# A looped TensorE program over a 256-column input ring, with one 120-row slot moved by gpsimd DMAs

## The chip, the cores and the metric

The kernel runs on one core of a Trainium2 chip. The metric is the device time of one execution in microseconds (us), lower is better. A profile shows one execution; its span is about 2 us below the measured time of the same execution.

An *engine* without a name is one of the 16 DMA engines of the profile's page; PE (TensorE), ACT (ScalarE), DVE (VectorE), POOL (GpSimd) and SP are the named ones. A *row* is the part of one SBUF partition that a DMA moves as one packet: 24,576 bytes for 64 columns of 192 bf16 channels. The trace's packet records give queue, time, duration and bytes, but no engine: which engine carried a row is always inferred here, from the 16 landings of a DMA and from its shape. "Over 4 engines" means that a DMA is written with `a` = 4 in `a c n`. The recorded texts speak of the *start* of such a gpsimd DMA, the engine on which it is taken to begin, and of moving it.

## The reference

A 1x1 grouped convolution: 512 x 512 pixels, 192 channels in 4 groups of 48. With a kernel of 1x1 it is one matrix product per group and pixel.

```python
# x: (1, 512, 512, 192) bf16, w: (1, 1, 4, 48, 48) bf16
xg = x.reshape(B, H, W, G, Cg)
out = einsum('bhwgc,gcd->bhwgd', xg, w[0, 0]).reshape(B, H, W, C)
```

100.66 MB are read and 100.66 MB are written, each byte once; the load and store queues of the kernel before fill 97.4% of the 16 engines' span with that, at 418 GB/s.

## The kernel before

Pixels lie on the partitions, `BIG` = 104 pixels ("columns") on each of 128 partitions per slot. SP loads slots into one ring of 520 columns; PE transposes four columns a "group" at a time, DVE copies the transposes to SBUF, PE multiplies, ACT writes the result over the input in the same ring, and stores go out from there on the ACT queue. A load waits for the store of the slot five before. PE's program is a Python loop, so each of its instructions exists once.

```python
BIG = 104
RCOLS = 5 * BIG
NARROW = ((0, 16), (32, 16))      # rows of the one narrow slot
NARROW_COLS = 48
NARROW_AT = (9,)
# ... cut

def transfers(ap, ring, p, c0=0, c1=None):
    c1 = c1 or p.size
    for (r0, rows, pix) in p.blocks:
        px = ap[pix:pix + rows * p.size, :]
        if p.full:
            view = px.rearrange("(p i) n -> p (i n)", p=rows)[:, c0 * C:c1 * C]
        else:
            view = px.rearrange("(c a i) n -> a c (i n)", a=4, c=rows // 4)
        yield view, ring[r0:r0 + rows, (p.at + c0) * C:(p.at + c1) * C]

# SP
for p in pieces:
    for q in pieces:
        if q.slot == p.slot - RCOLS // BIG:
            wq.wait(st_sem[q.i], st_val[q])
    for dram, sbuf in transfers(xf, ring, p):
        sp.dma_start(sbuf, dram).then_inc(ld_sem[p.i], 16)

# PE
for pair in range(NP):
    if pair + 1 < NP:
        transposes(pair + 1)
    matmuls(pair)
# ... cut
```

The narrow slot is there because the 16 engines are not equally fast (stores of 1.59 us instead of 1.476 on one of them, below). Its 32 rows go by DMAs over 4 engines, which by their shape leave the other 12 without work (no record names them); everything else is spread over all 16.

Of the kernel before, what the change touches and what calls it, by code (L numbers as in the profile page):

```python
# [6 lines left out]
BF16 = mybir.dt.bfloat16  # L7
# [4 lines left out]
C = GROUPS * CG  # L12
UC = 2 * C
# [11 lines left out]
BIG = 104  # L25
RCOLS = 5 * BIG
HEAD = (8, 20, 32)
LATE = 6
LATE_PARTS = (52, 52)
LAST_PARTS = (32, 32, 24, 16)  # L30
FULL = ((0, 128),)
NARROW = ((0, 16), (32, 16))
NARROW_COLS = 48
NARROW_AT = (9,)
NXP = 4
NXS = 3
# [3 lines left out]
class Waiter:  # L40

    def __init__(self, eng):
        self.eng = eng
        self.seen = {}
# [8 lines left out]
class Piece:  # L53

    def __init__(self, i, slot, at, g0, size, blocks, pix):
        self.i, self.slot, self.at, self.size = i, slot, at, size
        self.g0, self.g1 = g0, g0 + size // 4
        self.full = blocks is FULL
        self.blocks = []
        for (r0, rows) in blocks:  # L60
            self.blocks.append((r0, rows, pix))
            pix += rows * size
        self.pix_end = pix
        assert size % 4 == 0 and self.at + size <= RCOLS


def plan_pieces(npix):
    few = NARROW_COLS * sum(rows for _, rows in NARROW)
    at = [i for i in NARROW_AT if npix >= len(NARROW_AT) * few + 128 * (sum(HEAD) + BIG * (i + 2))]
    cols = (npix - few * len(at)) // 128  # L70
    assert cols % 4 == 0
    head = list(HEAD) if cols >= sum(HEAD) + BIG else []
    mid = cols - sum(head)
    slots = [[(BIG, FULL)]] * (mid // BIG) + ([[(mid % BIG, FULL)]] if mid % BIG else [])
    for i in at:
        slots.insert(i, [(NARROW_COLS, NARROW)])
    if head:
        slots.insert(0, [(s, FULL) for s in head])
    pieces, g, pix = [], 0, 0
    for n, parts in enumerate(slots):  # L80
        c = n * BIG % RCOLS
        for s, blocks in parts:
            pieces.append(Piece(len(pieces), n, c, g, s, blocks, pix))
            c, g, pix = c + s, pieces[-1].g1, pieces[-1].pix_end
    assert pix == npix
    return pieces


def bass_standalone__grouped__vision_kernel(nc, x, w, out):
# [3 lines left out]
    assert npix % 512 == 0, "the pixel count must be a multiple of 512"  # L93

    pieces = plan_pieces(npix)
    piece_of = {g: p for p in pieces for g in range(p.g0, p.g1)}
    NG = pieces[-1].g1
    NP = (NG + 1) // 2

# [4 lines left out]
    def groups(pair):  # L104
        return range(2 * pair, min(2 * pair + 2, NG))

    def transfers(ap, ring, p, c0=0, c1=None):
        c1 = c1 or p.size
        for (r0, rows, pix) in p.blocks:
            px = ap[pix:pix + rows * p.size, :]  # L110
            if p.full:
                view = px.rearrange("(p i) n -> p (i n)", p=rows)[:, c0 * C:c1 * C]
            else:
                view = px.rearrange("(c a i) n -> a c (i n)", a=4, c=rows // 4)
            yield view, ring[r0:r0 + rows, (p.at + c0) * C:(p.at + c1) * C]

    stores = []
    for p in pieces:
        late = pieces[-1].slot - p.slot
        parts = LAST_PARTS if late == 0 else LATE_PARTS if late < LATE else (BIG,)  # L120
        c = 0
        for n in parts if p.size == BIG and p.full else (p.size,):
            stores.append((p, c, c + n, p.g0 + (c + n) // 4))
            c += n
    st_val = {p: 16 * sum(len(p.blocks) for q, *_ in stores if q is p) for p in pieces}

    with ExitStack() as es:
        block = es.enter_context(nc.Block())
        ring = es.enter_context(nc.sbuf_tensor("ring", [128, RCOLS * C], BF16))
# [4 lines left out]
        wt = es.enter_context(nc.sbuf_tensor("wt", [128, WCOLS], BF16))  # L134
        xT_ps = es.enter_context(nc.psum_tensor("xT_ps", [128, NXP, 1024], BF16))
# [5 lines left out]
        ld_sem = [sem(f"ld{p.i}") for p in pieces]  # L141
        st_sem = [sem(f"st{p.i}") for p in pieces]
# [3 lines left out]
        e_done, fa_done = sem("e_done"), sem("fa_done")  # L146

        def columns(g):
            p = piece_of[g]
            at = p.at + 4 * (g - p.g0)  # L150
            return ring[:, at * C:(at + 4) * C]

        @block.gpsimd
        def _(gp):
            gp.memset(esel[:], 1.0).then_inc(p0_sem, 1)  # L155
            gp.memset(ident[:], 1.0).then_inc(p1_sem, 1)  # L156
            gp.wait_ge(p0_sem, 1)
            gp.affine_select(out=esel[:], in_=esel[:], pattern=[[-1, ECOLS]],  # L158
                             compare_op=AluOpType.is_equal, fill=0.0, base=ESHIFT,
                             channel_multiplier=1).then_inc(e_sem, 1)  # L160
            gp.wait_ge(p1_sem, 1)
            gp.affine_select(out=ident[:], in_=ident[:], pattern=[[-1, 128]],  # L162
                             compare_op=AluOpType.is_equal, fill=0.0, base=0,
                             channel_multiplier=1).then_inc(id_sem, 1)

        @block.sync
        def _(sp):
            wq = Waiter(sp)
            sp.dma_start(w_sb[:], wv).then_inc(w_sem, 16)  # L169
            for p in pieces:  # L170
                for q in pieces:
                    if q.slot == p.slot - RCOLS // BIG:
                        wq.wait(st_sem[q.i], st_val[q])
                for dram, sbuf in transfers(xf, ring, p):
                    sp.dma_start(sbuf, dram).then_inc(ld_sem[p.i], 16)  # L175

        @block.tensor
        def _(pe):
            wq = Waiter(pe)

            def build_weights():
                wq.wait(e_sem, 1)
                wq.wait(w_sem, 16)
                last = None
                for (tc, r, g, c0_) in WBLOCKS:
                    s0 = ESHIFT - r
                    col = WOFF[tc] + c0_
                    last = pe.matmul(o_ps[:, NOB - 1, col:col + CG], lhsT=esel[:, s0:s0 + 128],  # L188
                                     rhs=w_sb[:, g, :], start=True, stop=True, skip_group_check=True)
                last.then_inc(wb_sem, 1)  # L190

            def transposes(pair):
                wq.wait(e_done, pair - 1)
                last = None
                for g in groups(pair):
                    p = piece_of[g]
                    if g == p.g0:
                        wq.wait(ld_sem[p.i], 16 * len(p.blocks))
                    xg = columns(g)
                    for ul in range(2):  # L200
                        for tc in range(3):
                            j = ul * 3 + tc
                            last = pe.transpose(xT_ps[:, g % NXP, j * 128:(j + 1) * 128],  # L203
                                                xg[:, j * 128:(j + 1) * 128], ident[:])
                last.then_inc(t_done, 1)

            def matmuls(pair):
                wq.wait(e_done, pair + 1)
                for g in groups(pair):
                    xs = xT_sb[pair % NXS][:, g % 2 * 2 * UC:(g % 2 + 1) * 2 * UC]  # L210
                    wq.wait(fa_done, g - 1)
# [12 lines left out]
            wq.wait(id_sem, 1)  # L224
            transposes(0)
            wq.wait(wc_sem, 1)
            for pair in range(NP):
                if pair + 1 < NP:
                    transposes(pair + 1)
                matmuls(pair)  # L230

        @block.vector
        def _(dve):
# [3 lines left out]
            for pair in range(NP):  # L237
                n = len(groups(pair))
                b0 = pair * 2 % NXP
                wq.wait(t_done, pair + 1)  # L240
                wq.wait(mm_done, 2 * (pair - NXS + 1))
                dve.tensor_copy(xT_sb[pair % NXS][:, 0:n * 2 * UC].rearrange("p (g c) -> p g c", g=n),  # L242
                                xT_ps[:, b0:b0 + n, 0:2 * UC]).then_inc(e_done, 1)

        @block.scalar
        def _(act):
# [3 lines left out]
            def store():  # L250
                p, c0, c1, g1 = todo.pop(0)
                wq.wait(fa_done, g1)
                for dram, sbuf in transfers(of, ring, p, c0, c1):
                    act.dma_start(dram, sbuf).then_inc(st_sem[p.i], 16)  # L254

            for g in range(NG):
                wq.wait(mm_done, g + 1)
                v = 2 * g
                dst = columns(g).rearrange("p (u c) -> p u c", u=2)
                act.copy(dst, o_ps[:, v % NOB:v % NOB + 2, 0:UC]).then_inc(fa_done, 1)  # L260
                while todo and todo[0][3] <= g:
                    store()
            while todo:
                store()
            for p in pieces:
                wq.wait(st_sem[p.i], st_val[p])
# [28 lines left out]
```

## Time and profile before

485.38 us, median of 4 executions (485.06 to 485.62).

| what | value | where on the profile |
|---|---|---|
| span | 483.3 us | first line |
| load queue, store queue, instruction queue | 48.7%, 48.7%, 0.6% of 16 engines' span | part 3 |
| PE busy | 431.3 us, 89% | part 1 |
| PE waiting for loads | 21.1 us in 8 waits | wait list |
| the last chain of work | PE 54%, DMA 39% | part 4 |

These are lines of the profile's page: busy times, busy tenths in 40 equal slices of the span, GB/s per slice, the DMA queues (packets, MB, share of 16 engines) and the chain that ended last.

```profile
span 483.3 us, 13933 instructions
...
PE 431.3 (89%) x6262; PEld 392.1 (81%) x6262; DVE 250.2 (52%) x262; ACT 392.6 (81%) x522; POOL 1.3 (0%) x8
...
PE   5699999999999999998599999979998999999910
...
DMA  8999999999999999999999999999999999999993
GB/s 351 431 406 421 449 425 421 422 424 442 434 428 419 425 420 439 425 434 424 431 434 437 424 431 428 432 431 426 434 428 428 430 424 422 439 416 427 429 390 156
...
q10 hardware_dynamic: 4360, 100.67, 48.7%
q1 hardware_dynamic: 3416, 100.68, 48.7%
q8 instruction: 50, 0.82, 0.6%
...
PE 54%; DMA 39%; ACT 1%; issue 1%; SPq 0%; ACTq 0%
```

Between the first slice and the last two the engines are busy in every slice, at 406 to 449 GB/s. That is a kernel at its DMA limit. And from the wait list (waited for: us in total, times, longest):

```profile
PE xT_ps L203 <- DMA ring<-in_x_dram: 21.1, 8, 6.8
```

PE has little slack, but some: it waits for data, not data for it.

The trace also records every DMA packet with its start and duration. A row of 39,936 bytes takes 1.476 us in this kernel, and one of 24,576 bytes 0.912 us in the changed one (medians), which fits a few nanoseconds plus 0.03676 ns per byte. One engine takes about 8% longer for each row that it stores (1.587 us in the median instead of 1.476; which one, no record says). Chained by their times, the packets follow each other without gaps, so the time is the work of the engine that ends last (the prediction's chains end between 467 and 483.2 us of the 483.3).

### The profile page before, as it was taken

Reading aid. Unit: us, or ns where it says so; the run is one execution under the profiler, and the core shown is the slowest. Engines: PE = TensorE matmul, PEld = TensorE weight load, DVE = VectorE, ACT = ScalarE, POOL = GpSimd, SP = SyncE. Lnnn points to the kernel's source line nnn. Section 1 sums busy time; section 2 is a strip of 40 time slices with the busy share of each in tenths; the row PEclk is TensorE's granted clock in tenths of the full one; section 3 lists DMA queues with packets and bytes.
Section 4 is the critical chain, followed back from the end, with each engine's and each line's share of the span. In section 5 each row is a group of like instructions: output and inputs, shape, how many; then the busy total and the mean of one; then the engine's idle time right before and its main releaser. Section 6 shows DMA issues by size and latency. Waiting matters only on the chain.

```text
span 483.3 us, 13933 instructions
## 1 busy us (share of the span) xinstructions
PE 431.3 (89%) x6262; PEld 392.1 (81%) x6262; DVE 250.2 (52%) x262; ACT 392.6 (81%) x522; POOL 1.3 (0%) x8
## 2 busy tenths in 40 slices
PE   5699999999999999998599999979998999999910
PEld 5599888898898889887588988969787898899800
DVE  2345655656555565564256555544554655556500
ACT  2669999999999999998299999877888999999920
POOL 1000000000000000000000000000000000000000
PEclk9979999999999999999799999998999999999965
DMA  8999999999999999999999999999999999999993
GB/s 351 431 406 421 449 425 421 422 424 442 434 428 419 425 420 439 425 434 424 431 434 437 424 431 428 432 431 426 434 428 428 430 424 422 439 416 427 429 390 156
DMA packets 7834, 202.23 MB, mean 418 GB/s; under 512 B 1056, under 2 KB 1056, under 8 KB 1696
## 3 DMA queue, kind: packets, MB, share of 16 engines
q10 hardware_dynamic: 4360, 100.67, 48.7%
q1 hardware_dynamic: 3416, 100.68, 48.7%
q8 instruction: 50, 0.82, 0.6%
q14 instruction: 8, 0.07, 0.0%
HBM read 100.68 MB, written 100.66 MB: 417 GB/s over the span
## 4 chain that ended last, share of the span: by engine, by line
PE 54%; DMA 39%; ACT 1%; issue 1%; SPq 0%; ACTq 0%
PE o_ps L218 31%; PE xT_ps L203 22%; DMA ring<-in_x_dram 20%; DMA out_dram<-ring 19%; ACT ring L260 1%; SPq L175 0%; ACTq L254 0%; SPq L169 0%
## 5 line engine op out<-in xcount | busy, mean ns | idle before, releaser
L260 ACT CAST ring<-o_ps 128x768 bf16<-128x768 f32 x521 | 391.3, 802 | 68.5 <-PE o_ps L218 61.0
L242 DVE COPY xT_sb<-xT_ps 128x1536 bf16<-128x1536 bf16 (+1 forms) x261 | 249.6, 956 | 206.0 <-PE xT_ps L203 206.0
L218 PE MATMUL o_ps<-wt,xT_sb 128*128 128x144 bf16 (+1 forms) x3126 | 292.0, 236 | 5.9 <-ACT ring L260 1.3
L218 PEld LDWEIGHTS o_ps<-wt,xT_sb 128*128 128x128 bf16 x3126 | 212.0, 99 | 43.4 <-ACT ring L260 30.2
L203 PE MATMUL xT_ps<-ident,ring 128*128 128x128 bf16 x3126 | 222.7, 221 | 21.1 <-DMA ring<-in_x_dram 21.1
L203 PEld LDWEIGHTS xT_ps<-ident,ring 128*128 128x128 bf16 x3126 | 191.1, 99 | 22.7 <-DMA ring<-in_x_dram 19.8
L188 PE MATMUL o_ps<-w_sb,esel 48*128 48x48 bf16 x10 | 0.6, 210 | 2.7 <-DMA w_sb<-in_w_dram 2.7
L188 PEld LDWEIGHTS o_ps<-w_sb,esel 48*128 48x128 bf16 x10 | 0.5, 113 | 2.6 <-POOL esel L158 2.6
L236 DVE CAST wt<-o_ps 128x480 bf16<-128x480 f32 x1 | 0.7, 658 | 3.3 <-PE o_ps L188 3.3
L260 ACT ACT_TABLE_LOAD x1 | 1.3, 1283 | 0.8 <-PEq L280 0.8
L158 POOL TENSOR_SCALAR_AFFINE_SELECT esel<-esel 48x272 bf16<-48x272 bf16 x1 | 0.4, 405 | 0.0
L155 POOL MEMSET esel<- 48x272 bf16 x1 | 0.3, 318 | 0.3 <-POOLq L280 0.3
L162 POOL TENSOR_SCALAR_AFFINE_SELECT ident<-ident 128x128 bf16<-128x128 bf16 x1 | 0.3, 285 | 0.0
L156 POOL MEMSET ident<- 128x128 bf16 x1 | 0.2, 198 | 0.0
L280 POOL MEMSET const-bfloat16-1.0<- 128x1 bf16 x1 | 0.1, 102 | 0.0
L280 POOL MEMSET const-uint8-127<- 128x1 uint8 x1 | 0.1, 102 | 0.0
L280 POOL MEMSET const-float32-0.0<- 128x1 f32 x1 | 0.1, 98 | 0.3 <-issue 0.3
L280 POOL MEMSET const-float32-1.0<- 128x1 f32 x1 | 0.1, 98 | 0.0
## 6 DMA issues: line engine op xcount, KB each, us to landing
ring<-in_x_dram SPq DMA_DIRECT2D x19, 4992.0 KB, 37.5
out_dram<-ring ACTq DMA_DIRECT2D x13, 4992.0 KB, 45.5
out_dram<-ring ACTq DMA_DIRECT2D x10, 2496.0 KB, 47.7
out_dram<-ring ACTq DMA_DIRECT2D x3, 1536.0 KB, 19.7
ring<-in_x_dram SPq DMA_DIRECT2D x1, 1536.0 KB, 8.4
out_dram<-ring ACTq DMA_DIRECT2D x1, 1152.0 KB, 16.6
ring<-in_x_dram SPq DMA_DIRECT2D x1, 960.0 KB, 5.2
out_dram<-ring ACTq DMA_DIRECT2D x1, 960.0 KB, 28.6
```

Of the source, the lines that this page charges most:

```text
L155: gp.memset(esel[:], 1.0).then_inc(p0_sem, 1)
L156: gp.memset(ident[:], 1.0).then_inc(p1_sem, 1)
L158: gp.affine_select(out=esel[:], in_=esel[:], pattern=[[-1, ECOLS]], compare_op=AluOpType.is_equal, fill=0.0, base=ESHIFT, channel_multipli ...
L162: gp.affine_select(out=ident[:], in_=ident[:], pattern=[[-1, 128]], compare_op=AluOpType.is_equal, fill=0.0, base=0, channel_multiplier=1) ...
L188: last = pe.matmul(o_ps[:, NOB - 1, col:col + CG], lhsT=esel[:, s0:s0 + 128], rhs=w_sb[:, g, :], start=True, stop=True, skip_group_check=True)
L203: last = pe.transpose(xT_ps[:, g % NXP, j * 128:(j + 1) * 128], xg[:, j * 128:(j + 1) * 128], ident[:])
L218: last = pe.matmul(o_ps[:, v % NOB, c0_:c1_], lhsT=xs[:, j * 128:(j + 1) * 128], rhs=wt[:, WOFF[tc]:WOFF[tc] + (c1_ - c0_)], start=(tc == ...
L236: dve.tensor_copy(wt[:], o_ps[:, NOB - 1, 0:WCOLS]).then_inc(wc_sem, 1)
L242: dve.tensor_copy(xT_sb[pair % NXS][:, 0:n * 2 * UC].rearrange("p (g c) -> p g c", g=n), xT_ps[:, b0:b0 + n, 0:2 * UC]).then_inc(e_done, 1)
L260: act.copy(dst, o_ps[:, v % NOB:v % NOB + 2, 0:UC]).then_inc(fa_done, 1)
L280: nc = _bacc.Bacc("TRN2", target_bir_lowering=False, num_devices=1)
```

## The change

Intent: give PE a short program that is looped, so that PE's instructions are not fetched all the time by the same DMA engines (50 packets of 16,384 bytes here, 0.966 us in the median, the row after each about 0.4 us longer); separate the input ring from the output ring (each 4 slots of 64 columns), so that a load waits for the transposes rather than for a store; and replace the old narrow slot by one of 120 rows, which 15 engines are to carry and the slow one is not.

To leave one engine out, gpsimd DMAs are used. Slot 17 is made of DMAs over 4, 3 and 8 engines, twice (rows 0-15, 20-31 and 64-95; then 32-47, 52-63 and 96-127), and between the first and second of each three a small copy, the *spin*, is to shift the engines of the next DMA by one, past the slow one.

```diff
-BIG = 104
-RCOLS = 5 * BIG
-NARROW = ((0, 16), (32, 16))
-NARROW_COLS = 48
-NARROW_AT = (9,)
+SLOT = 64
+NSLOT = 4
+LAP = NSLOT * SG
+NARROW = 17
+NARROW_ROWS = ((0, 16, 4), (16, 0, 1), (20, 12, 3), (64, 32, 8),   # (first row, rows, a); 0 rows: spin
+               (32, 16, 4), (48, 0, 1), (52, 12, 3), (96, 32, 8))
...
+            for s in slots:                       # gpsimd
+                if not s.narrow:
+                    continue
+                wq.wait(t_done, 8 * (s.n - NSLOT + 1))
+                for dram, sbuf in narrow_parts(xf, ring_in, s):   # dram: "(c a i) n -> a c (i n)", a = engines
+                    if dram is None:
+                        wq.wait(spin_sem, 16 * spins)
+                        spins += 1
+                        gp.dma_start(spin[0:1, 0:64], xf[0:1, 0:64]).then_inc(spin_sem, 16)
+                    else:
+                        gp.dma_start(sbuf, dram).then_inc(nl_sem, 16)
+                wq.wait(nl_sem, 16 * NDMA)
+                gp.sem_inc(ld_sem[s.n % NSLOT][0], 16)
+                wq.wait(mm_done, s.g1 + 2)
+                ... the same again for the store of the slot
...
-            for pair in range(NP):
-                if pair + 1 < NP:
-                    transposes(pair + 1)
-                matmuls(pair)
+            with pe.Fori(0, NLAP):
+                for pair in range(LAP // 2):
+                    if pair:
+                        pe.wait_ge(e_done, pair)
+                    nxt = (pair + 1) % (LAP // 2)
+                    ...
+                    transposes(nxt, (2 * nxt, 2 * nxt + 1))
+                    matmuls(pair, (2 * pair, 2 * pair + 1))
+                pe.sem_inc(e_done, -(LAP // 2))
+                pe.sem_inc(fa_done, -LAP)
```

## The prediction

> **What bounds the kernel.** DMA, all 16 engines. The page's queue table gives loads 48.7%, stores 48.7% and instruction fetch 0.6% of the 16 engines' span: 98% of 483.3 us busy, 418 GB/s. The compute engines have slack: PE 431 us busy, ACT 391, DVE 250; the wait list shows PE waiting only 21 us for loads; a pair of groups takes 1.63 us where PE runs freely (timeline), so 261 pairs need about 425 us. The trace's packet records follow each other on an engine without a gap, so I could chain them (roughly) into engines: idle time is nil until an engine's last packet. From the span's start, three engines end at about 467 us, most at 475 to 478, the last ones at 480, 481 and 483.2. The time is the work of the slowest DMA engine; the mean is 476.
>
> **What makes engines unequal** (same records):
> - 50 instruction fetches of 16,384 bytes (0.88 to 1.12 us, plus about 0.4 us on the next row)[...].[...]
> - One engine stores its 39,936-byte rows in about 1.59 us instead of 1.476: an estimated 16 us over the run.
> - The old narrow slot gives 4 engines 11 us of extra work.
>
> **The change.** The PE program falls from 6262 matmults (each a weight load and a matmul) to 796, a loop body of about 1580 instructions run 8 times: [...]nearly all fetches vanish. The narrow slot now loads 15 engines and spares the slow one. Per row the engine's cost fits 5 ns + 0.03676 ns per byte (1.473 us for 39,936 bytes, 0.739 for 19,968). Ordinary engines then carry 12.61 MB, 467 us, against 462 for the three idle-early engines now: they end near 472. The slow engine carries 12.21 MB, about 10 us less: it ends near 473.5. Added: more packets (under 1 us), one or two wait instructions per pair on PE, a branch per lap[...], 16 small gpsimd DMAs. Separate rings let loads be issued when transposed instead of stored; DMA is saturated already, so that gains nothing itself. Unprofiled time is 2.3 us above the span: 476 to 478.
>
> **Two doubts.**
> 1. The loop may be fetched again each lap: [...]482 to 485.
> 2. The small "spin" DMA is lowered as 16 x 4 elements.[...] the slow engine gets the extra work too, and the time is 486 to 491. No run yet shows it.
>
> **What would show it.** Right: instruction queue below 10 packets; q1 and gpsimd rows on 15 engines, spin as one engine's packets; all engines end within 3 us of each other; DMA 9 tenths in all but the last slice; chain of waits still mostly DMA and PE. Wrong: 50 or more fetches; PE gaps of microseconds every lap; one engine running alone for 10 us at the end; PE idle not on loads but on ACT, or DMA slices below 9 near the end (output ring of 256 columns too small).
>
> I predict 478 us, range 474 to 488. Faster by over 2% (below 475.9) 0.28, within 2% 0.66, slower 0.06.

The sum: the slow engine's end, 473.5 us, and 2.3 us of an unprofiled execution over the span make 475.8; with up to 2 us for a branch per lap, whose cost no trace gave, it came to 476 to 478. (In the changed kernel PE is idle for 0.20 and 0.19 us where its laps begin at 386.3 and 439.8 us.) Cut from the first doubt is how the fetches spread over the engines. The traces give their total: 50 fetches of 0.966 us and 0.398 us (medians) on the row after each are an estimated 68 us of engine time, 4.3 us on each engine if all 16 share it. Cut from the second doubt is the reason why the spin might not pass over the slow engine, and then "the slow engine gets the extra work too"; it came from no trace.

## The result, and the profile after

498.5 us, median of 4 executions (496.26 to 501.31); 485.38 us before on the same chip. The ratio is 1.0274, with a 95% interval of 1.0228 to 1.0321: slower. (A ratio is the mean time of one kernel's fast runs over that of the other's of the same rounds, so it is not quite the ratio of the medians quoted.) The prediction's range ended at 488.

The same lines of the page, for the changed kernel; POOL's busy tenths and the gpsimd queue q0 are new. The profiled execution is the slowest of the four, 501.31 us.

```profile
span 499.6 us, 13884 instructions
...
PE 429.4 (86%) x6172; PEld 390.8 (78%) x6172; DVE 246.8 (49%) x258; ACT 389.1 (78%) x514; POOL 10.2 (2%) x24
...
PE   4999999999988899886830999972999999999995
...
POOL 1000000000000000210000021000000000000000
...
DMA  8999999999999999999999789999799999999986
GB/s 326 426 412 426 439 421 429 437 437 425 429 437 434 424 431 437 431 413 419 419 394 372 306 317 339 406 411 405 293 392 429 434 429 435 427 426 428 425 343 274
...
q1 hardware_dynamic: 5104, 97.73, 47.3%
q10 hardware_dynamic: 5616, 97.72, 46.1%
q0 software_dynamic: 1088, 5.90, 3.1%
q8 instruction: 6, 0.10, 0.1%
...
PE 8%; ACT 3%; issue 0%; ACTq 0%
```

Three things stand out. The instruction queue fell from 50 packets to 6, all of them between 19 and 64 us, so the loop is not fetched again each lap. The loss is in one place: the slices of 12.5 us from number 21 to 30 (250 to 375 us) show 293 to 411 GB/s where 420 to 440 is usual, while slot 17 is loaded and stored. And in the first of them (394 and 372 GB/s) DMA still shows nine tenths and more: the engines are busy but move less. PE runs out of input at about that time ("6830", numbers 19 to 22 of its row), and only after that do the engines run dry ("78", numbers 23 and 24). At the store it is the same again: PE's "72" in 27 and 28, the engines' "7" in 29.

The wait list gives the second half of it.

```profile
POOL ring_in L186 <- PE xT_ps L242: 199.5, 1, 199.5
...
PE xT_ps L242 <- issue: 28.9, 6, 21.6
POOL spin L184 <- DMA spin<-in_x_dram: 17.5, 1, 17.5
PE o_ps L257 <- ACT ring_out L313: 15.0, 17, 12.0
...
ACT ring_out L313 <- DMA out_dram<-ring_out: 12.4, 1, 12.4
```

The gpsimd loads are issued from 201.5 us on and have all landed only at 275.1 us (semaphore landings of the trace), 73.6 us later; the ordinary slots of this kernel land 35.0 us after their issue (median). PE stands for 21.6 us in one piece before slot 17 (the list calls it "issue", because gpsimd and not a DMA raises that semaphore). Later ACT waits 12.4 us for slot 17's store before it may write slot 21, and PE 12.0 us for ACT. From 346 us on PE has no pause over 0.3 us, and the end is now PE's: its last matmul ends at 494.3 us, 4 us before the last store row (498.7), where in the kernel before 21 us lie between the two (461.0 and 482.3). The engines stay busy until about 475 us and have too little to do after that (343 and 274 GB/s). The chain that ended last does not tell this: it breaks off after 11% of the span, here and in most kernels with two rings, e5 and e20 among them.

An account of the loss can be made from the packet records: for each stretch, 16 engines times its length, less the recorded packet time, is *idle*; recorded packet time less 8 ns and 0.03676 ns per byte of each packet is *excess*, that is, slowness. In undisturbed stretches of this kernel both are near zero (within 3 engine-us in 20 us).

```
changed kernel, engine-us        excess   idle
200 to 275 us (load of slot 17)    62.9   -4.1
275 to 350 us (its store)          75.9  106.7
350 to 375 us                      30.5   52.9
200 to 375 us                     169.3  155.5
```

So the engines lose about 325 engine-us, 20 us each, half because their packets are slow and half because they have nothing to do. Most of the slowness is in ordinary rows: of the 169.3 engine-us of excess 116.5 are in the SP loads, 27.4 in the ACT stores and 25.4 in the gpsimd rows, of which 74 of 240 take over 0.95 us. The experiments ask for the cause of each half.

### The profile page after: what moved, and what is told of

The parts are those of the page before. It is cut to its first block, busy times and chain, and to the rows that moved or that the text cites. A ratio compares the mean times of both kernels' runs of the same rounds, so it can differ in the third digit from the quotient of the medians.

```text
span 499.6 us, 13884 instructions
## 1 busy us (share of the span) xinstructions
PE 429.4 (86%) x6172; PEld 390.8 (78%) x6172; DVE 246.8 (49%) x258; ACT 389.1 (78%) x514; POOL 10.2 (2%) x24
## 5 line engine op out<-in xcount | busy, mean ns | idle before, releaser
L313 ACT CAST ring_out<-o_ps 128x768 bf16<-128x768 f32 x513 | 387.9, 801 | 105.2 <-PE o_ps L257 86.1
L290 DVE COPY xT_sb<-xT_ps 128x1536 bf16<-128x1536 bf16 x257 | 246.1, 958 | 243.2 <-PE xT_ps L242 243.2
L257 PE MATMUL o_ps<-wt,xT_sb 128*128 128x144 bf16 (+1 forms) x3078 | 286.4, 236 | 20.5 <-ACT ring_out L313 15.0
L242 PE MATMUL xT_ps<-ident,ring_in 128*128 128x128 bf16 x3084 | 220.1, 222 | 41.6 <-issue 28.9
L242 PEld LDWEIGHTS xT_ps<-ident,ring_in 128*128 128x128 bf16 x3084 | 189.7, 100 | 44.3 <-issue 44.2
L186 POOL DMA_DIRECT2D ring_in<-in_x_dram x6 | 3.5, 594 | 199.5 <-PE xT_ps L242 199.5
L196 POOL DMA_DIRECT2D out_dram<-ring_out x6 | 3.4, 563 | 70.7 <-PE o_ps L257 70.7
L184 POOL DMA_DIRECT2D spin<-in_x_dram x2 | 1.0, 514 | 17.5 <-DMA spin<-in_x_dram 17.5
L194 POOL DMA_DIRECT2D spin<-in_x_dram x2 | 1.0, 510 | 8.2 <-DMA spin<-in_x_dram 8.2
## 6 DMA issues: line engine op xcount, KB each, us to landing
out_dram<-ring_out POOLq DMA_DIRECT2D x2, 768.0 KB, 23.9
```

The source lines that it names most:

```text
L184: gp.dma_start(spin[0:1, 0:64], xf[0:1, 0:64]).then_inc(spin_sem, 16)
L186: gp.dma_start(sbuf, dram).then_inc(nl_sem, 16)
L194: gp.dma_start(spin[0:1, 0:64], xf[0:1, 0:64]).then_inc(spin_sem, 16)
L196: gp.dma_start(dram, sbuf).then_inc(st_sem[s.n], 16)
L242: last = pe.transpose(xT_ps[:, g % NXP, j * 128:(j + 1) * 128], xg[:, j * 128:(j + 1) * 128], ident[:])
L257: last = pe.matmul(o_ps[:, v % NOB, c0_:c1_], lhsT=xs[:, j * 128:(j + 1) * 128], rhs=wt[:, WOFF[tc]:WOFF[tc] + (c1_ - c0_)], start=(tc == ...
```

## The experiments

Eighteen kernels were run. All gave the right result except e15. All times are of fast runs where nothing else is said (the state of e15's single run is unknown), beside the kernel before on the same chip at 485.1 to 485.5 us. The expectations name theories by letters: **G**, gpsimd DMAs as such slow the others; **S**, the wait for the spin does it; **T**, a gpsimd DMA over few engines costs every engine many turns, so the load is late; **P**, a slot's rows are slow, and slow the rows beside them, when it is cut into DMAs that give engines other rows than a 128-row DMA does. P is the reading of shapes and durations; no record names an engine, and why such rows should be slow is not shown.

### The parts of the new slot

**e1_hw120**: the 120 rows as one 15-engine DMA on the SP queue and one on the ACT queue; no gpsimd.

```diff
-        view = ap[s.pix:s.pix_end, :].rearrange("(p i) n -> p (i n)", p=128)[:, c0 * C:c1 * C]
-        return view, ring[:, (s.at + c0) * C:(s.at + c1) * C]
+        rows = NROWS if s.narrow else 128
+        view = ap[s.pix:s.pix_end, :].rearrange("(p i) n -> p (i n)", p=rows)[:, c0 * C:c1 * C]
+        return view, ring[0:rows, (s.at + c0) * C:(s.at + c1) * C]
... (the gpsimd DMAs go; SP and ACT no longer skip the narrow slot)
```

> The narrow slot of 120 rows is loaded by one SP DMA and stored by one ACT DMA (15 engines); no gpsimd DMA is left. Theory G (the gpsimd DMAs of this slot are slow, PE waits 22 us for the load and ACT 12 us for the store, and the lead that is lost comes back as a PE-bound tail): DMA at 9 tenths in all slices, no PE wait over 7 us after the start, at most 490 us. Within theory G, if one slow-storing engine sets the end (it is not spared here): 486 to 490, all other engines done 10 us earlier; if it does not, 475 to 480. Rival R (the rings of 256 columns or the loop cost the time, not the gpsimd DMAs): 494 to 500 as in the changed kernel.

Measured: 500.64 us, ratio 1.0306 [1.0289, 1.0324]. There is no gpsimd DMA in this kernel and it is as slow as the changed one, so G is not needed to explain it. Excess while slot 17 is loaded (200 to 275 us): 52.8 engine-us. By its shape this DMA gives 120 rows to 15 engines instead of 128 to 16; which engine has which of them, no record shows. From 200 to 375 us the excess is 91.9 engine-us, against 10.1 in e5 (below): (91.9 - 10.1) / 16 = 5.1 us per engine, about half of the 10.6 us that e1 is over e5. The last engine fell up to 16 us behind the others in its loads.

**e2_no_spin**: the changed kernel without its spins and the waits for them.

```diff
-NARROW_ROWS = ((0, 16, 4), (16, 0, 1), (20, 12, 3), (64, 32, 8),
-               (32, 16, 4), (48, 0, 1), (52, 12, 3), (96, 32, 8))
+NARROW_ROWS = ((0, 16, 4), (20, 12, 3), (64, 32, 8),
+               (32, 16, 4), (52, 12, 3), (96, 32, 8))
```

> The changed kernel without its four spin DMAs; the twelve gpsimd row DMAs stay. Theory T (each tiny descriptor of a gpsimd DMA, about 3 per engine and DMA, waits one turn behind a 24,576-byte row of each of the two other queues, about 1.83 us a turn): a quarter fewer DMAs, load of the slot down from 67 us to about 50, PE stall down from 22 us to below 10, time 486 to 493. Rival S (the delay is POOL waiting 17.5 us for the spin DMA to land): stall gone, 476 to 490 like the run without gpsimd DMAs. Rival D[...]: unchanged, 496 to 501.

Measured: 498.82 us, 1.0285 [1.0268, 1.0303]; load 66.6 us from first issue to last landing instead of 73.6, longest PE stall 16.8 us instead of 21.6. S falls: the wait costs some us of the load and nothing of the total. But T missed as well (load about 50 us, 486 to 493 us), and the number fits D, the expectation's last rival; e1 speaks against any delay of gpsimd DMAs as the cause, since it is as slow without any. Looking back, this run said more than I took from it: taking the spins out did not change the total, which fits spins that had done nothing.

**e3_one_gp**: the same 120 rows as one 15-engine gpsimd DMA each way (`NARROW_ROWS = ((0, 120, 15),)`).

> The narrow slot by one gpsimd DMA of 120 rows each way, no spins. Theory T: about 3 + 8 turns of 1.83 us, so the load lands some 20 to 25 us after issue, before PE needs it (about 40 us), no PE stall; time as in the run without gpsimd DMAs within 3 us. Rival (any gpsimd DMA starves here): load still over 45 us and time above 494.

Measured: 502.1 us, 1.0344 [1.0303, 1.0384]. The load landed after 36.4 us, half of the changed kernel's 73.6, and still PE stalled 18.5 us, because now slot 16's ordinary load came late: excess in 200 to 275 us was 162.3 engine-us. Fewer turns do not help where rows are slow. This spoke for P.

**e4_hw120_unrolled**: e1 with a Python loop in place of the looped PE program (`for _lap in range(NLAP)` for `with pe.Fori(0, NLAP)`).

> The run without gpsimd DMAs, with PE's loop unrolled by the host language (same waits, 50 instruction fetches again). If the fetches cost only engines that are not the last to finish: same time within 2 us. If the loop is what helps: 6 to 10 us slower than the looped one. If the loop hurts PE: faster.

Measured: 495.29 us, 1.0197 [1.0176, 1.0218], with 49 instruction fetches. The slow rows are there without the loop too (excess from 200 to 375 us 83.1 engine-us, e1 91.9). But this kernel is 5 us faster than e1, which is the recorded outcome "if the loop hurts PE", and that is not explained. (With full slots, below, the loop changes nothing.)

### Full slots: what is left without a narrow slot

**e5_full_slots**: 32 slots of 128 rows and a 4-column tail that is loaded and computed but not stored; no gpsimd DMA.

```diff
-        narrow = n == NARROW
-        size = SLOT if narrow else min(SLOT, (npix - pix) // 128)
-        slots.append(Slot(n, size, narrow, pix))
+        slots.append(Slot(len(slots), SLOT, False, pix))
+    slots.append(Slot(len(slots), 4, False, 0))   # loaded and computed again, not stored
... (the gpsimd DMAs go)
```

> No narrow slot at all: 32 full slots of 128 rows (the last 4 columns are loaded and computed again, not stored, since the loop's last lap transposes one pair ahead), no gpsimd DMA. Theory E (one engine stores about 8 per cent slower than the others; it carries 2050 of 2048 columns here against 2036 in the kernel before, and sets the end): the last engine to land a load falls steadily behind the second last, from below 1 us to about 16 us, and the time is 487 to 492. Then the gpsimd slot costs the changed kernel the rest, about 8 us. Rival R (rings or loop cost it): 494 to 500. If neither: below 484.

Measured: 490.0 us (489.82 to 490.09), 1.0094 [1.0077, 1.011], as expected. GB/s of its 40 slices:

```profile
GB/s 318 436 408 433 425 439 425 433 433 427 437 425 442 423 435 431 429 435 423 445 423 444 423 433 429 423 443 423 445 423 431 431 427 431 432 425 427 410 277 24
```

There is no dip before the end, so the rings and the loop make none; the loss is at the end, where one engine is left alone. The last of the 16 landings of one store shows how it gets there: it comes 9.1 us after the first at 240 us and 14.9 us at 390 us, while the other 15 stay within 4 us. This is the slow engine, in a kernel without any gpsimd DMA.

**e13_full_unrolled**: e5 with the Python loop.

> The full-slot run with PE's loop unrolled by the host language: 49 or 50 fetches[...] again. If the slow-storing engine[...] sets the end: 489 to 491.5, same as looped. If fetches were on the critical path: 495 or longer. If the loop hurts PE: below 488.

Measured: 489.66 us, 1.0092 [1.0075, 1.0109]. The looped program and its 6 fetches instead of about 50 gain nothing here, because the slow engine sets the end.

**e14_before_no_narrow**: the kernel before with `NARROW_AT = ()`.

> The kernel before without its own narrow slot (2048 columns on every engine instead of 2036 on twelve of them). Theory E: the slow-storing engine gets 12 columns more, 12 x 0.226 us = 2.7 us, so 487.5 to 489.5; the new rings and the loop then cost the rest up to 490. Rival (the narrow slot of before does nothing): 485 to 486.5.

Measured: 487.18 us, 1.0038 [1.0022, 1.0055]. The old narrow slot had been worth about 2 us (2.7 were expected, so the time lies just below the range).

### A slot in two halves, and a gpsimd DMA of 128 rows

**e11_halves**: e5 with slot 17 as two 64-row DMAs each way, on SP and ACT. By the shape each of the sixteen engines has four rows of each DMA instead of eight of one, so the engines may share out the rows in another way; no record shows it.

```diff
-        return view, ring[:, (s.at + c0) * C:(s.at + c1) * C]
+        for r0 in (0, 64) if s.n == HALVES else (0,):      # HALVES = 17
+            r1 = r0 + (64 if s.n == HALVES else 128)
+            yield view[r0:r1, :], ring[r0:r1, (s.at + c0) * C:(s.at + c1) * C]
... (SP and ACT issue one DMA for each)
```

> The full-slot run with slot 17 loaded and stored by two DMAs of 64 rows instead of one of 128, all from SP and ACT: same bytes[...]. Theory P[...]: rows of slot 17 clearly above 0.912 us (up to 1.8), records in that stretch exceed their nominal time by 60 engine-us or more on the load, as in the runs with 120 contiguous rows, and the time is 3 to 10 us longer than with full slots, without any gpsimd DMA. Rival W (gpsimd DMAs are slow in themselves): 490 as with full slots.

Measured: 496.38 us (496.2 to 496.71), 1.0228 [1.0211, 1.0245]: 6.4 us over e5, with the same bytes on the same two queues. Slices 19 and 20 fall while slot 17 is loaded and 24 and 25 while it is stored:

```profile
GB/s 319 432 422 414 434 424 437 435 423 437 429 431 434 425 438 437 423 433 373 359 425 430 433 383 410 427 435 429 433 429 428 439 433 423 432 424 428 367 303 32
```

Of the 38 load rows that start between 230 and 235 us, all take over 1.02 us, 1.60 us in the mean, where 0.912 us is usual. The excess from 200 to 375 us is 105.5 engine-us, against 10.1 in e5: (105.5 - 10.1) / 16 = 6.0 us per engine, which is nearly all of the 6.4.

**e12_gp128**: e5 with slot 17 as one 128-row gpsimd DMA each way (16 engines, rows shared out as in the hardware queues' DMAs, by the shape).

> The full-slot run with slot 17 by one gpsimd DMA of 128 rows each way: 16 engines, each its usual rows, no spins, no row left out. Theory P: no excess, load landed in 20 to 25 us, no PE wait over 6 us, 489 to 492 as with full slots. Rival W: excess of 60 engine-us or more and 494 or longer.

Measured: 489.72 us, 1.0091 [1.0074, 1.0107], the same as e5, with no dip:

```profile
GB/s 321 432 406 431 429 427 435 431 433 431 433 429 431 435 425 437 431 433 431 431 435 427 435 431 431 431 435 429 431 433 427 435 433 432 429 421 427 409 275 24
...
q0 software_dynamic: 288, 6.29, 3.0%
```

PE's longest wait was 8.8 us, over the 6 expected, and cost nothing. G has fallen for a DMA over 16 engines, and P holds as far as it can be seen without engine numbers in the records: this gpsimd slot in one DMA cost nothing (489.72 us beside 490.0), and e11's slot in two halves cost 6.4 us (496.38).

### Other spins, tried too early

**e8_early_spin1**: the narrow slot as slot 3, so that a late load would have time; the spins copy one element each, which the trace shows as one data packet per spin (the 64-element spin is 16 packets of 8 bytes). **e9_early_spin16** has the 64-element spins in the same place, **e10_early_spin1_unrolled** is e8 with the Python loop. In e8 and e10 the wait between spins goes as well, and in all three SP fills the eight rows that nobody loads (16-19 and 48-51) with two small DMAs.

```diff
-NARROW = 17
+NARROW = 3
...
-                        gp.dma_start(spin[0:1, 0:64], xf[0:1, 0:64]).then_inc(spin_sem, 16)
+                        gp.dma_start(spin[0:1, spins:spins + 1], xf[0:1, spins:spins + 1]).then_inc(spin_sem, 16)
```

> The changed kernel with the narrow slot as slot 3, so that its gpsimd load starts at once and PE needs it only 40 us later, and with spin DMAs of one element[...].[...] the late engine is at most 4 us behind the second last through the run, and the time is 475 to 481, faster than the kernel before.[...]

> As the previous one, with the spin DMAs of the changed kernel (64 elements, 16 packets[...] in its trace).[...] the slow engine gets the extra rows: late engine up to 16 us behind, 486 to 492.[...]

> The run with early narrow slot and one-element spins, PE's loop unrolled by the host language: 50 instruction fetches[...]. If that slot spares the slow engine[...]: 5 to 8 us slower than the looped one. If the slow engine still sets the end: within 2 us.

Two conditions and one rival are cut from these. e8: if the one-element spin does not shift the engines, or not past the slow one, 486 to 492 us. e9: its two outcomes are for spins that leave the engines as they are (486 to 492) and for spins that shift them (the time of e8).

Measured: 507.55 us (1.0457), 503.46 us (1.042; the median of its three fast runs, 505.88 with the slow one) and 507.6 us (1.0459). A clear miss: I took a spin that is one packet for a spin that shifts the engines by one. In e8 the excess from 10 to 50 us alone was 190.8 engine-us, 12 us per engine, so its rows were not right either. The loop again made no difference (e8 and e10). What moves the start was still open.

### Tries to move the start

**e15_probe_start**: slots 5 to 20 each loaded by four gpsimd DMAs of 32 rows over 8 engines, followed by one one-element copy; stores as always, so the rows of these slots are permuted and the result is wrong. If each one-element copy shifts the engines of the DMAs after it, the rows of the sixteen slots must differ in their durations.

```diff
+            for j, n in enumerate(range(5, 21)):
+                for r0 in (0, 64, 32, 96):
+                    gp.dma_start(ring_in[r0:r0 + 32, ...], px.rearrange("(c a i) n -> a c (i n)", a=8, c=4))
+                gp.dma_start(spin[0:1, j:j + 1], xf[0:1, j:j + 1])
```

> Full slots; slots 5 to 20 are loaded by four gpsimd DMAs of 32 rows over 8 engines each, then one one-element DMA; stores as always, so the result is wrong on purpose (rows permuted within these slots). Theory P[...] one slot of the sixteen (or two[...]) has row packets near 0.91 us[...]; the others have means of 1.1 us and more. If the start is not moved by the one-element DMAs, all sixteen slots look alike, within 5 per cent.[...] Time 490 to 620 us, of no interest.

(A third outcome: all rows near 0.91 us.)

Measured: one look, 550.87 us, of no interest. Most slots could not be read: the load waits for the transposes in this kernel, the engines had run dry, and the first row of each burst on an idle engine mostly took 1.3 to 2 us, wherever it lay. But two slots, fourteen spins apart, were loaded beside busy hardware loads: in slot 5 all 128 gpsimd rows took under 0.95 us, in slot 19 126 of 128 did (mean 0.913 and 0.914 us). Neither of the two outcomes that I had written down fits, because idle engines spoiled the reading. What fits these two slots is that their rows lie alike, and well, in both: the fourteen one-element copies between them shifted nothing. Slot 6, one spin after slot 5, agrees: 124 of its 128 rows took under 0.95 us. The other thirteen slots had means of 1.13 to 1.19 us; that idle engines are the reason for them is argued, not shown.

**e16_start_right**, **e18_start_one_off**, **e17_96_rows**, **e19_spins_repaired**: four tries to move the start by a multi-engine copy. In e16 the two DMAs over 4 engines (rows 0-15 and 32-47) go by the hardware queues and gpsimd has the 3- and 8-engine DMAs, each pair after a copy over 5 partitions. e18 is e16 with 4 partitions in the first copy and two more copies (9 and 8) at the end. e17 leaves out the rows of the 3-engine DMAs (20-31 and 52-63) as well and uses copies over 8 partitions. e19 is the changed kernel with copies over 9 and 8 partitions for each spin.

```diff
 e16, e18
-NARROW_ROWS = ((0, 16, 4), (16, 0, 1), (20, 12, 3), (64, 32, 8), ...)
+NARROW_ROWS = ((0, 16, 4), (32, 16, 4),                            # SP and ACT queues
+               (0, 0, 5), (20, 12, 3), (64, 32, 8), (0, 0, 5), (52, 12, 3), (96, 32, 8))   # gpsimd
-                        gp.dma_start(spin[0:1, 0:64], xf[0:1, 0:64]).then_inc(spin_sem, 16)
+                        gp.dma_start(spin[0:k, 8 * spins:8 * spins + 8], xf[0:k, 0:8]).then_inc(spin_sem, 16)
 e19
+                        for k in (9, 8):
+                            gp.dma_start(spin[0:k, 8 * spins:8 * spins + 8], xf[0:k, 0:8]).then_inc(spin_sem, 16)
```

> Changed kernel; slot 17's rows[...] go by the SP and ACT queues (4-engine DMAs), the rest by gpsimd DMAs of 3 and 8 engines, and the start is moved by tiny DMAs of 5 engines[...]. Theory P[...]:[...] excess in the packet records of 200 to 275 us under 10 engine-us (after: 63), load done in 40 to 50 us, PE stall under 8 us, 477 to 485 us. If the start is not what matters: as the changed kernel less two DMAs, 492 to 499 us, and equal to e18.

> e16 with its first tiny DMA over 4 engines in place of 5[...]. Theory P: excess of 40 engine-us or more around the load and again at the store, 489 to 498 us, at least 4 us above e16. If the start is not what matters: equal to e16 within 1.5 us.

> e16 with the rows[...] left out as well (96 rows; only 8-engine gpsimd DMAs, tiny DMAs of 8 engines), the last slot 16 columns. Fewer turns for the load: 25 to 35 us, no PE stall at it. Theory P: 478 to 485 us. If the start is not what matters: 488 us or more.

> Changed kernel with each spin as two tiny DMAs of 9 and 8 engines[...] in place of the 16-engine one and its wait; nothing else. Theory P:[...] excess is gone (under 15 engine-us at the load, after 63), the load still takes 60 to 70 us for its many turns and PE still stalls 15 to 22 us; 486 to 493 us. If the start is not what matters: 497 to 500 us.

| run | us | ratio | excess 200 to 275 us | longest PE stall |
|---|---|---|---|---|
| e16 | 492.93 | 1.017 [1.0145, 1.0195] | 77.8 | 7.0 |
| e18 | 493.12 | 1.0157 [1.0136, 1.0178] | 82.7 | 7.0 |
| e17 | 490.05 | 1.0098 [1.008, 1.0116] | 41.0 | 7.7 |
| e19 | 500.6 | 1.031 [1.0272, 1.0348] | 75.3 | 25.7 |

All four missed, and e16 equals e18, as I had written for "the start is not what matters". But the excess was there in all four, so rows were slow in all of them, and e17 gives a hint why. These are the 16 landings of one load late in the run, in us after the first of them (from the trace's semaphore landings):

```
e17, load at 362 to 386 us:  0.0 0.1 0.1 0.3 1.2 2.1 3.0 3.7 3.8 4.0 7.9 19.0 20.4 23.2 23.7 24.5
```

Had the slot spared four engines, as it was written to, four landings would be ahead of twelve. Instead eleven are ahead and five are behind, by 11 to 17 us (19.0 and more against 7.9). That fits gpsimd rows that all 16 engines share alike, eight in one DMA and eight in the other; four engines that have the rows of the hardware queues on top; and the slow engine as the fifth straggler, not spared. It is a reading of the landings: no record names an engine. So e16 and e18 may be nearly the same kernel in effect (their excess at the store still differs, 12.8 and 33.5 engine-us from 275 to 350 us, which this does not explain), and no copy tried so far shows that it shifted anything, whether it was one element, 64 elements or 4, 5, 8 or 9 short rows: e15's left fast rows fast, the others left slow rows slow. In e17 the two row DMAs over 8 engines seem to have different engines, by this reading, with only such a copy between them; so the row DMAs may shift the engines where the copies do not. They differ in their pattern, three dimensions (`a c n`) against two, and in their size.

**e20_spin_as_rows**: e16 with its spins written like the row DMAs.

```diff
-                        gp.dma_start(spin[0:k, 8 * spins:8 * spins + 8], xf[0:k, 0:8]).then_inc(spin_sem, 16)
+                        px = xf[0:2 * k, :].rearrange("(c a) n -> a c n", a=k, c=2)
+                        gp.dma_start(spin[0:2 * k, C * spins:C * (spins + 1)], px).then_inc(spin_sem, 16)
```

> e16 with its four spins written as row DMAs are (pattern a c n, 5 engines of two 384-byte rows) in place of the plain 5-row copy. If the row DMAs' pattern is what moves the start:[...] excess in the packet records of 200 to 275 us under 10 engine-us (e16: 77); the engine that stores slowly has no rows of slot 17, so that after the narrow store no load lands with five engines far behind; PE stall at slot 17 under 8 us; 477 to 485 us. If spins don't move it in any form: as e16, 492 to 495 us, five engines 20 us behind.[...]

(A third outcome: excess of 40 engine-us or more and 488 us or more.)

Measured: **477.45 us** (477.31 to 479.07, 5 runs) beside 485.12 us of the kernel before; ratio 0.9849 [0.9835, 0.9862]: clearly below 1. It is 15.5 us faster than e16, from which it differs in four tiny DMAs alone, and it beats both kernels. These four changed in pattern and in size: each has five packets, of 768 bytes instead of 16, and no run separates the two. GB/s of e16, and then lines of e20's page:

```profile
GB/s 324 432 408 429 432 423 439 425 439 425 439 425 437 427 435 427 429 391 380 384 407 435 429 429 427 427 427 433 425 433 427 437 427 434 424 423 423 357 319 135
```

```profile
span 475.7 us, 13884 instructions
...
PE   4999999999898888988889899949999999999991
...
DMA  8999999999999999999999999999999999999997
GB/s 324 429 406 426 428 430 428 438 438 430 430 428 433 430 430 432 428 432 428 432 438 433 432 430 429 428 424 430 438 434 428 430 432 428 427 436 419 428 428 295
...
q0 software_dynamic: 768, 4.34, 2.2%
```

No slice is lower than 406 GB/s between the first and the last. All 176 gpsimd rows take 0.912 us. The excess from 200 to 375 us is 12.4 engine-us (e16: 93.5, the changed kernel: 169.3). Late in the run (380 to 435 us) the 16 landings of a store come within 2.3 to 4.1 us; of a load one comes up to 3.8 us before the other fifteen, which fits an engine that was spared. At the end all engines finish within 4.2 us, at 471.0 to 475.2 us. From its POOL timeline (start, duration, what was waited for), and its wait list:

```profile
1.92 0.73 POOL L185 DMA_DIRECT2D spin<-in_x_dram  x1
202.49 1.10 POOL L190 DMA_DIRECT2D ring_in<-in_x_dram  x2 [199.84 <-PE xT_ps L253]
203.59 0.56 POOL L185 DMA_DIRECT2D spin<-in_x_dram  x1
204.13 1.10 POOL L190 DMA_DIRECT2D ring_in<-in_x_dram  x2
251.33 0.55 POOL L185 DMA_DIRECT2D spin<-in_x_dram  x1 [46.10 <-DMA ring_in<-in_x_dram]
```

```profile
PE o_ps L268 <- ACT ring_out L329: 11.9, 21, 6.6
PE xT_ps L253 <- issue: 11.8, 7, 2.1
...
ACT ring_out L329 <- DMA out_dram<-ring_out: 7.0, 1, 7.0
```

The load of slot 17 takes 48 us now, and no PE stall of a load is longer than 2.1 us. The late store still holds ACT for 7.0 us; PE has the slack for that.

## Why the prediction was wrong, point by point

- **"The time is the work of the slowest DMA engine": right for the kernel before, not for the changed one.** e5, which has no narrow slot, ends with a slice of 24 GB/s, a sixteenth or so of the usual 430 (430 / 16 = 27), that is, by this estimate, with about one engine alone for some 12 us; and e20, which by its landings spares one, is 12.5 us faster than e5. The changed kernel itself is ended by PE, whose stalls at slot 17 made it late (last matmul at 494.3 us).
- **"Nearly all fetches vanish": right**. 6 fetches instead of 50. That this gains time by itself is not shown: e5 and e13 are equal (490.0 and 489.66 us), because the slow engine hides it.
- **"The narrow slot now loads 15 engines and spares the slow one": this is the step that failed.** The spins as written did nothing that shows (e2 without them, 498.82 us, is as slow as the changed kernel's 498.5), and the form of the spins decides (e16 and e20 differ in them alone, 492.93 and 477.45 us). By the author's reading the rows were thus not on the engines that they were costed for. This was doubt 2 of the prediction, seen for a good reason: the trace shows 16 packets of 8 bytes for each spin. But it was left as a doubt when it was the decisive step of the whole change.
- **"The slow engine gets the extra work too, and the time is 486 to 491": too small by 7.5 to 12.5 us, because two costs were missing from the sum.** The first is slow rows. The 16 rows of the first gpsimd load all take 0.912 us; after it (217.9 us on) rows of slot 17 and ordinary rows slow down: excess of 169 engine-us, most of it in the ordinary loads (116.5). That the rows lay on other engines than in a 128-row DMA (P) fits e11, e12 and e20; why that slows them is not shown. The second is the stall. "Separate rings let loads be issued when transposed", so slot 17 was issued only 52 us before PE was ready for it (201.5 and 253.7 us), and its load took 73.6 us. "16 small gpsimd DMAs" were costed as packets of under 1 us in all; their turns were not counted. Each gpsimd DMA over few engines has small packets beside its rows: 48 packets of 4 bytes beside 32 rows over 8 engines, 64 beside 16 rows over 4, 68 beside 12 rows over 3, 16 for each spin (784 in all on the changed kernel's gpsimd queue). A turn is 1.82 us here, two rows of 0.912. A DMA of four rows per engine is five turns, an estimated 9 us; six of them are an estimated 55 us. The six of e2's load landed 8.2 to 11.8 us after one another, which agrees.
- **The sum agrees with the traces.** Against e20, the changed kernel has 169.3 - 12.4 = 156.9 engine-us more excess and 155.5 + 14.4 = 169.9 more idle time from 200 to 375 us (e20's idle comes out at -14.4, the error of the method). Divided by 16 that is 20.4 us. The two traced executions differ by 499.6 - 475.7 = 23.9 us (the medians by 21.05); counted the same way, 3.3 us of it come after 375 us, where PE's lateness leaves the engines idle. This is bookkeeping: it says where the time went, and not why. Of e16's 15.5 us, (93.5 - 12.4) / 16 = 5.1 us are slow rows; the rest is idle time after 375 us, that is, uneven work, with five engines ending up to 10 us after the others.
- **"I predict 478 us": e20 has 477.45 us.** That is the slot as it was meant, with 32 of its rows moved by the hardware queues. Its last landings, 471.0 to 475.2 us, agree with the 472 and 473.5 that the prediction had for the ends of its engines. The cost model for engines that carry what they are meant to carry was right; what was wrong, by the author's reading, was which engines the DMAs would run on.

What the runs do not show: which engine carries which row, and so P itself beyond its durations and landings, and which property of e20's spins matters, their three dimensions or their size. Nor do they show why some times scatter: the changed kernel's by 1% (496.26 to 501.31 us), and those of e2, e3 and e19 too, while four of e20's five lie within 0.2 us; e1 scatters without gpsimd. If the engines of the first gpsimd DMA differ from one execution to the next, the readings above, each of one traced execution, need not hold for others; no run tested it. It is also not shown that a version with all its rows on gpsimd and the right spin would be as fast as e20; it would have six row DMAs in the load (66.6 us in e2, where e20's load takes 48), and the stall of the late load might be longer.

## What to carry to other kernels

When a change depends on which DMA engine carries which rows, check exactly that first, with a kernel that does only this: the durations of single rows in the packet records (0.912 us against 1.0 to 1.6 us here) and the spread of the 16 landings of one later DMA tell it at a glance, where GB/s and busy shares only show that something is slow. A busy DMA with falling GB/s (nine tenths busy at 394 and 372 GB/s here) meant slow packets, and a suspect to test is a slot that is cut into other DMAs than its neighbours, as here (e11: load rows of 1.60 us in the mean instead of 0.912). A load of many gpsimd DMAs over few engines needs time for its turns (8 to 12 us for each DMA of four rows per engine here); compare that with how early it can be issued.
